# A transformer block on one core: ten fill products give way to 194 products of 28 rows and 12 of 32 columns

## The chip, the core and the metric

The kernel runs on one core of one Trainium2 chip. A core has five engines that work side by side: TensorE (PE in the profile; PEld is its loading of weights), VectorE (DVE), ScalarE (ACT), GpSimd (POOL) and SyncE (SP), which here issues DMAs. The metric is the device time of one execution in microseconds (us); less is better. TensorE multiplies a stationary operand (the weights, loaded first, up to 128 rows by 128 columns) with a moving operand of up to 512 columns, and writes into PSUM, which has eight banks of 128 partitions by 512 f32 values.

## What is computed

One block on 2048 tokens of width 448: a conditioning vector gives shifts, scales and gates; then attention with 16 heads of 28, and a gated MLP that mixes tokens with a 2048x2048 matrix.

```python
mod = (silu(c) @ w_mod).reshape(1, 6, 1, -1)
sa, ca, ga, sb, cb, gb = (mod[:, i] for i in range(6))
h = layernorm(x) * (1 + ca) + sa
x = x + ga * A(h, wqkv, wo)               # softmax attention, 16 heads of 28
h = layernorm(x) * (1 + cb) + sb
x = x + gb * B(h, w_in, w_sp, b_sp, w_out) # gelu, layernorm of one half, w_sp over tokens
```

The change lies in the first line of `h`: the layernorm of the first tokens, ahead of everything that TensorE has to do.

## The kernel before

Tokens are worked on in four groups of 512 (four tiles of 128). For each group the normalised tokens are transposed, scaled and shifted into `hT`, split into a high and a low part, and multiplied with the weights for V (`pv`), Q and K (`pq`). Then come the attention over 16 heads (`mt`, row maxima; `st_ps`, scores; `o_ps`, probabilities times V), the output projection and the MLP.

All engines follow the order in which the code is written out; nothing is moved by a scheduler. Each engine takes its instructions in that order and waits for semaphores of the others where data are not there. PSUM banks are handed out by `bank(name)`, which takes the first of the list `banks` and puts it at the end.

At the start (lines as in the profile of before):

- POOL sets constants to zero or one: `wv`, a part of `heapF` and the last columns of `V` (L297 to L299).
- `pe_fill(21, ones)` (L316) is the first thing in TensorE's queue: 21 products of a tile of ones with itself, 128x128, into a bank `wu` that nobody reads. Another one comes a little later.
- Meanwhile VectorE takes the statistics of the first four tiles of x (`ln_stat`, L368), POOL computes the reciprocal deviations `rs` (L166, L167), and VectorE normalises (`xn`, L379).
- `tp_first` (L460) transposes `xn` on TensorE into four banks `tps`. `mod_dot` (L484, L486) sums the conditioning products into `pc`, from which `mod_cols` (L497, VectorE) takes the columns `col_ca` and `col_sa`.
- `h_hi` (L534, ScalarE) applies these columns to the transposed tiles, and `v_step` (L554) multiplies the result.

Four kinds of product matter below. Products of `heapF`, `heapD` and `heapA` are in the type f32r, which takes one pass. Products of `ones`, `P` and `V` are in full f32, where one product leaves two records in the trace. Transpositions are products with a unit matrix. `o_ps` (L775) has 32 output partitions a product; four of them, one for each quarter of the 128 output partitions, stand in a row:

```python
pe.matmul(otile[h][32 * qb : 32 * qb + 32, :], V[:, kt, h, :], ptiles.pop((u, qb)), start=kt == 0, stop=kt == NT - 1)
```

No product of this kernel has fewer than 128 rows.

Of the kernel before, what the change touches and what calls it, by code (L numbers as in the profile page):

```python
# [8 lines left out]
F32 = mybir.dt.float32  # L9
# [80 lines left out]
def tile_adaln_mha_gmlp(ctx, tc, x, wqkv, wo, w_in, w_spT, b_sp, w_out, cT, w_mod, out):  # L90
    nc = tc.nc
    ctx.enter_context(tc.manual_schedule())
    pe, dve, act, pool, sp = nc.tensor, nc.vector, nc.scalar, nc.gpsimd, nc.sync
# [15 lines left out]
    ones = const.tile([128, 128], F32, name="ones")  # L109
# [5 lines left out]
    cols = {}  # L115
# [5 lines left out]
    heapF = dpool.tile([128, 4 * 896], F32R, name="heapF", tag="heapF")  # L121
    dpool.tile([128, 104], F32, name="padD")

    def hview(heap, off, a, b):
        return heap[:, off : off + a * b].rearrange("p (a b) -> p a b", b=b)
# [104 lines left out]
    V = vpool.tile([128, NT, H, 32], F32, name="V")  # L230
# [12 lines left out]
    banks, mode = list(range(7)), [None]  # L243

    def bank(name):
        k = mode[0](name) if mode[0] else banks[0]
        banks.remove(k)
        banks.append(k)
        return ring.tile([128, 512], F32, name=name, tag=f"b{k}")
# [64 lines left out]
    def pe_fill(n, with_):  # L314
        for _ in range(n):
            pe.matmul(wu[:, 0:128], with_[:, 0:128], ones, start=True, stop=True)  # L316

    accs = {}

    def mod_acc(pair, k):  # L320
# [42 lines left out]
    def ln_stat(g, ts):  # L363
        if g not in mv1:
            mv1[g] = e1.tile([128, 4, 2], F32, name="mv"), e1.tile([128, 4], F32, name="rs")
        for t in ts:
            st = e1.tile([128, 6], F32, name="st", bufs=4)
            dve.bn_stats(out=st, in_=xts[4 * g + t])  # L368
            dve.bn_aggr(out=mv1[g][0][:, t, :], in_=st)
# [82 lines left out]


    tps, fs = {}, {}
    for c in (0, 2, 1, 3):
        tps[c] = bank("tp")

    def tp_first(t, cs=(0, 2, 1, 3)):
        for c in cs:
# [38 lines left out]
                out=cols[nm][:, c : c + 1], in0=pcs[c][:, part * 128 : part * 128 + 1], scalar1=plus1, scalar2=None, op0=ALU.add  # L498
            )

    pe_fill(21, ones)
    ln_stat(0, (0, 1))
    ln_rs(0, 0, 2)
    ln_stat(0, (2, 3))
# [592 lines left out]
    h = H - 1  # L1097
# [49 lines left out]
    heapF = dpool.tile([128, 4 * 896], F32R, name="heapF", tag="heapF")  # L1147
# [260 lines left out]
    for s in range(2):  # L1408
        for six in (False, True):
            prev = None  # L1410
            for n in [n for n in range(s, NP, 2) if PRODUCTS[n][1] or not six]:
                c, _, new, _ = PRODUCTS[n]
# [253 lines left out]
```

## Time and profile before

| | us |
|---|---|
| runs shown (2), lowest and highest | 1376.22, 1376.56 |
| median | 1376.39 |
| profiled execution, span from its first to its last instruction | 1375.3 |
| TensorE busy with products in that span | 1370.1 |
| TensorE's wait for its first operand, at the start | 1.0 |
| ScalarE's wait for the first `xn` (`acc` L471 behind `xn` L379) | 4.5 |

Of the profiled execution the trace gives the span; no other time of it is listed. In the profile an engine's busy time is the union of its instructions. Products overlap on TensorE, so that the record of one is longer than the distance to the next; what a product costs in a dense row is read from the distance of starts. "Idle before" a group is the time in which the engine had nothing to do ahead of it, with the instruction that ended the wait. The chain of waits is followed backwards from the last instruction, at each step to what released it. A window lists, for each engine, its busy time and in brackets the records that fall into it; then the granted clock of TensorE, the share of the DMA engines and their rate.

### The profile page before, as it was taken

The page shows a single profiled execution, that of the slowest core. Times are in us where ns is not written, and L with a number is a line of the kernel's source. Part 1 is how long each engine was busy: PE and PEld are TensorE (multiplying, and loading weights), DVE is VectorE, ACT ScalarE, POOL GpSimd, SP SyncE. Part 2 cuts the span into 40 slices and gives each one's busy share as a digit, 9 for nine tenths or more (in the row PEclk, how much of TensorE's full clock was granted, in tenths as well). Part 3 has the DMA queues.
Part 4 walks back from the last instruction along what each step waited for, and adds up shares of the span by engine and source line. Part 5 has one row for each costly group of instructions (what it writes and reads, how often), then busy time and mean ns, then how long its engine had stood idle before and what let it go on. Part 6 is the DMA issues. An engine that isn't in the chain of part 4 may idle for free.

```text
span 1375.3 us, 20071 instructions
## 1 busy us (share of the span) xinstructions
PE 1370.1 (100%) x7088; PEld 973.9 (71%) x7088; DVE 1069.3 (78%) x1729; ACT 789.5 (57%) x1466; POOL 356.1 (26%) x358
## 2 busy tenths in 40 slices
PE   9999999999999999999999999999999999999998
PEld 8888655555555555555555554888898888888898
DVE  8898888888888888888888880662268798889682
ACT  6623666676767676767777779364234754444221
POOL 2144334243335544633442302200142000000000
PEclk9999999999999999999999999999999999999999
DMA  8464642455244534552343321533202433335842
GB/s 296 138 177 176 187 118 85 109 161 153 69 117 138 151 121 124 156 148 77 110 126 88 96 57 50 174 142 126 85 1 77 130 100 115 115 93 180 270 158 83
DMA packets 93345, 174.65 MB, mean 127 GB/s; under 512 B 17016, under 2 KB 32250, under 8 KB 90698
## 3 DMA queue, kind: packets, MB, share of 16 engines
q1 hardware_dynamic: 90526, 169.07, 40.9%
q10 hardware_dynamic: 2718, 4.30, 0.9%
q8 instruction: 56, 0.92, 0.3%
q14 instruction: 45, 0.37, 0.1%
HBM read 111.71 MB, written 56.82 MB: 123 GB/s over the span
## 4 chain that ended last, share of the span: by engine, by line
PE 97%; DVE 1%; ACT 0%; issue 0%; DMA 0%; POOL 0%; DVEq 0%; ACTq 0%
PE st_ps L760 19%; PE acc L1442 19%; PE o_ps L775 17%; PE mt L728 17%; PE z_ps L1334 5%; PE z_ps L1166 5%; PE pq L415 4%; PE wo_ps L1031 3%; PE y_ps L1522 2%; PE y_ps L1521 2%; PE y_ps L1520 2%; PE pv L397 2%; PE tp L193 1%; DVE st L368 0%; PE pv L554 0%
## 5 line engine op out<-in xcount | busy, mean ns | idle before, releaser
L733 DVE TENSOR_REDUCE pm<-mt 128x1 f32<-128x512 f32 x1024 | 631.3, 682 | 85.9 <-PE mt L728 85.8
L764 ACT ACTIVATE P<-st_ps 128x512 f32<-128x512 f32 x1024 | 514.4, 630 | 201.8 <-PE st_ps L760 201.8
L760 PE MATMUL st_ps<-qst,kst 128*128 128x512 f32 x1024 | 404.3, 406 | 0.0
L728 PE MATMUL mt<-kst,qst 128*128 128x512 f32 x1024 | 402.5, 393 | 0.1
L760 PEld LDWEIGHTS st_ps<-qst,kst 128*128 128x128 f32 x1024 | 191.2, 188 | 141.4 <-issue 93.1
L775 PE MATMUL o_ps<-P,V 128*32 128x512 f32 x2048 | 247.1, 598 | 0.0
L1442 PE MATMUL acc<-wsp_h,heapA 128*128 128x512 f32 x752 | 231.5, 389 | 0.0
L728 PEld LDWEIGHTS mt<-kst,qst 128*128 128x128 f32 x1024 | 192.4, 188 | 32.0 <-POOL kst L665 0.5
L882 POOL TENSOR_TENSOR ws_raw<-ws_raw 128x512 f32<-128x512 f32 x124 | 159.3, 1288 | 195.7 <-DMA ws_scr<-ws_raw 138.9
L1442 PEld LDWEIGHTS acc<-wsp_h,heapA 128*128 128x128 f32 x752 | 141.1, 188 | 29.2
L1442 PE MATMUL acc<-wsp_l,heapA 128*128 128x512 f32 x376 | 146.3, 389 | 0.0
L775 PEld LDWEIGHTS o_ps<-P,V 128*32 128x32 f32 x2048 | 54.7, 109 | 122.9 <-issue 114.6
L1222 ACT ACTIVATE wsp_h<-raw_sp 128x512 fp32r<-128x512 f32 x104 | 65.6, 632 | 125.7 <-PE acc L1442 111.2
L143 DVE TENSOR_TENSOR wsp_l<-raw_sp,wsp_h 128x512 fp32r<-128x512 f32 x104 | 70.4, 687 | 16.6 <-ACT wsp_h L1222 16.4
L1442 PEld LDWEIGHTS acc<-wsp_l,heapA 128*128 128x128 f32 x376 | 70.6, 188 | 14.7
L415 PE MATMUL pq<-heapD,heapD 128*128 128x512 f32 x196 | 61.8, 390 | 0.0
L1338 DVE BATCH_NORM_STATS2 stz<-z 128x6 f32<-128x448 f32 x32 | 19.9, 626 | 44.6 <-ACT z L1337 44.5
L143 DVE TENSOR_TENSOR heapA<-z,heapA 128x1536 fp32r<-128x1536 f32 (+2 forms) x25 | 39.9, 1605 | 6.6 <-ACT heapA L1257 6.5
L1337 ACT ACTIVATE z<-z_ps 128x448 f32<-128x448 f32 x32 | 17.4, 543 | 47.4 <-PE z_ps L1334 47.4
L415 PEld LDWEIGHTS pq<-heapD,heapD 128*128 128x128 f32 x196 | 36.7, 188 | 7.4
L804 POOL TENSOR_TENSOR osb<-osb,rb 128x512 f32<-128x512 f32 x15 | 19.3, 1287 | 85.6 <-DMA rb<-r_scr 80.8
L1521 PE MATMUL y_ps<-wouts,uT 128*128 128x448 f32 x112 | 40.9, 365 | 0.0
(231 smaller groups left out, 1432.1 us busy)
## 6 DMA issues: line engine op xcount, KB each, us to landing
ws_scr<-ws_raw SPq DMA_DIRECT2D x92, 256.0 KB
raw_sp<-ws_scr SPq DMA_DIRECT2D x92, 256.0 KB
ws_raw<-in_w_spT_dram SPq DMA_DIRECT2D x72, 256.0 KB
kst<-qk_scr SPq DMA_DIRECT2D x45, 224.0 KB
qst<-qk_scr SPq DMA_DIRECT2D x45, 224.0 KB
qk_scr<-qh SPq DMA_DIRECT2D x28, 256.0 KB
qk_scr<-ql SPq DMA_DIRECT2D x28, 256.0 KB
z_scr<-z1t SPq DMA_DIRECT2D x28, 256.0 KB
```

The lines of the kernel that those rows point to most:

```text
L143: eng.tensor_tensor(out=dst, in0=a, in1=hi.bitcast(F32), op=ALU.subtract)
L415: pe.matmul(pq, wqk[:, b, m * 128 : (m + 1) * 128], hT[g][:, a, :], start=j == 0, stop=j == NST - 1)
L728: pe.matmul(mt, qst[h % 3][:, t * 128 : (t + 1) * 128], kst[h % 3][:, kb * 512 : (kb + 1) * 512], start=True, stop=True)
L733: dve.tensor_reduce(out=pms[h][:, t, kb : kb + 1], in_=mt, axis=AX.X, op=ALU.max)
L760: pe.matmul(st, kst[h % 3][:, kt * 128 : (kt + 1) * 128], qst[h % 3][:, qb * 512 : (qb + 1) * 512], start=True, stop=True)
L764: act.activation(p, st, AF.Exp, scale=SCALE)
L775: pe.matmul(otile[h][32 * qb : 32 * qb + 32, :], V[:, kt, h, :], ptiles.pop((u, qb)), start=kt == 0, stop=kt == NT - 1)
L882: pool.tensor_tensor(out=ws_tile(op[0]), in0=ws_tile(op[2]), in1=ws_tile(op[4]), op=ALU.add if op[3] == "+" else ALU.subtract)
L1166: pe.matmul(ps_t, w1[:, b, f * 128 : (f + 1) * 128], h2T[g][:, a, :], start=j == 0, stop=j == NST - 1)
L1334: pe.matmul(ps_t[:, :D], h2T[g][:, a, tt * 128 : (tt + 1) * 128], w2[:, b, hf * D : (hf + 1) * D], start=j == 0, stop=j == NST - 1)
L1442: pe.matmul(a[j], z[:, c], w, start=start and k == 0, stop=st == 3 and k == 2, skip_group_check=not new or j == 3)
L1521: pe.matmul(y[:, :D], uT[k][:, 7 + f, ts], wouts[0][:, f, :], start=False, stop=False)
```

## The change

Three things change, all at the start.

Two memsets are added to POOL's queue: 1024 columns of `heapF` to 0.5, and the first 512 columns of `V` to 1.0. Both places are written again later, by the weights for Q and K and by the first V tile.

`pe_fill(21, ones)` becomes `pe_fill(11, ones)`, and behind it stands `probe()`, whose results nobody reads. It takes four banks and issues, from those constants:

- 24 fours of products of 28 rows, 128 weight columns and 512 moving columns, type f32r. The i-th of a four takes partitions 32i to 32i+27 and writes bank i.
- Three times: four products of 32 output partitions in full f32 (`cols`, with the weights and the moving operand from `V`, all 128 rows), then six more fours.
- Two products of 28 rows and 256 columns, on the third and fourth quarter, then six more fours.

Then the list of banks is set so that the transpositions get the banks that they had.

```diff
+    pr = hview(heapF, 0, 2, 512)
+    pool.memset(heapF[:, 0:1024].bitcast(F32), 0.5)
+    pool.memset(V[:, 0, :, :], 1.0)
+
+    def probe():
+        pt = [bank("probe") for _ in range(4)]
+
+        def mm(k, i, rows, src):
+            r = slice(rows * i, rows * i + (28 if rows == 32 else rows))
+            pe.matmul(pt[k], src[r, 0, 0:128], src[r, 1, :], start=True, stop=True)
+
+        def quads(n, src):
+            for _ in range(n):
+                for i in range(4):
+                    mm(i, i, 32, src)
+
+        def cols():
+            for half in range(1):
+                for i in range(4):
+                    pe.matmul(pt[0][32 * i : 32 * i + 32, :], pv[:, 0:32], pv, start=True, stop=True)
+
+        pv = V[:, 0:2, :, :].rearrange("p a h d -> p (a h d)")[:, 0:512]
+        quads(24, pr)
+        for _ in range(3):
+            cols()
+            quads(6, pr)
+        for i in (2, 3):
+            r = slice(32 * i, 32 * i + 28)
+            pe.matmul(pt[i][:, 0:256], pr[r, 0, 0:128], pr[r, 1, 0:256], start=True, stop=True)
+        for _ in range(6):
+            for i in (0, 1, 2, 3):
+                mm(i, i, 32, pr)
+
...
     tps, fs = {}, {}
-    for c in (0, 2, 1, 3):
-        tps[c] = bank("tp")
...
-    pe_fill(21, ones)
+    pe_fill(11, ones)
+    probe()
+    banks[:] = [1, 2, 3, 4, 5, 6, 0]
+    for c in (0, 2, 1, 3):
+        tps[c] = bank("tp")
     ln_stat(0, (0, 1))
```

TensorE's queue from its start to the first product of the V weights, before (line, operation, output and inputs, shape of the output, count; `wu` is the fill bank, `tp` the transposed x, `pc` the conditioning sums):

```order
L316 MATMUL wu<-ones 128x128 x21
L460 MATMUL tp<-ident,xn 128x128 x8
L484 MATMUL pc<-silu,wm 128x2
L486 MATMUL pc<-ones,acc 128x128 x2
L460 MATMUL tp<-ident,xn 128x128 x8
L316 MATMUL wu<-ones 128x128
```

The same place now, up to the first transpositions; line numbers behind the new function are higher by 31 or more:

```order
L316 MATMUL wu<-ones 128x128 x11
L327 MATMUL probe<-heapF 128x512 x96
L337 MATMUL probe<-V 32x512 x4
L327 MATMUL probe<-heapF 128x512 x24
L337 MATMUL probe<-V 32x512 x4
L327 MATMUL probe<-heapF 128x512 x24
L337 MATMUL probe<-V 32x512 x4
L327 MATMUL probe<-heapF 128x512 x24
L346 MATMUL probe<-heapF 128x256 x2
L327 MATMUL probe<-heapF 128x512 x24
L491 MATMUL tp<-ident,xn 128x128 x8
```

The 206 products stand between the fill and the first transposition. The first `probe` product of `heapF` and the first of `V` each wait for POOL, and the first transposition into each bank now also waits for the product that wrote the bank before it.

POOL's queue at the same place, the one piece of the difference that isn't a line number:

```order
 L298 MEMSET heapF 64x896
 L299 MEMSET V 128x256x4
+L319 MEMSET heapF 128x1024
+L320 MEMSET V 128x512
 L166 TENSOR_SCALAR rs<-mv 128x2
 L167 TENSOR_TENSOR rs<-rs,mhalf 128x2
```

The two memsets stand ahead of the first reciprocal deviation `rs`. The queues of VectorE, ScalarE and SyncE keep their order.

## The prediction

> **What bounds the kernel now.** I read the page first, for the engine that carries the end:
>
> ```profile
> span 1375.3 us, 20071 instructions
> PE 1370.1 (100%) x7088; PEld 973.9 (71%) x7088; DVE 1069.3 (78%) x1729; ACT 789.5 (57%) x1466; POOL 356.1 (26%) x358
> PE 97%; DVE 1%; ACT 0%; issue 0%; DMA 0%; POOL 0%; DVEq 0%; ACTq 0%
> ```
>
> TensorE (PE) is 97% of the chain that ended last. Whatever makes it later early on comes out at the end nearly whole, unless a wait behind that place takes it up. So only the place of the change matters, the first microseconds. The timeline there, PE first, then its weight loads (PEld), POOL and ScalarE (columns: start, length, engine, line, output and inputs, count, idle before and its releaser):
>
> ```profile
> 8.00 1.34 PE L460 MATMUL tp<-ident,xn 128*128 128x128 f32 x8
> 9.18 0.28 PE L484 MATMUL pc<-silu,wm 128*128 128x2 f32 x2
> 9.47 0.71 PE L486 MATMUL pc<-ones,acc 128*128 128x128 f32 x4
> 10.02 1.06 PE L460 MATMUL tp<-ident,xn 128*128 128x128 f32 x8
> ...
> 8.57 0.53 PEld L460 LDWEIGHTS tp<-ident,xn 128*128 128x128 f32 x5 [0.33 <-ACT xn L389]
> ...
> 2.71 0.96 POOL L299 MEMSET V<- 128x1024 f32 x1
> 6.08 0.24 POOL L166 TENSOR_SCALAR rs<-mv 128x2 f32<-128x2 f32 x1 [2.42 <-DVE mv L369]
> ...
> 10.69 0.78 ACT L534 ACTIVATE heapD<-tp,col_sa,col_ca 128x512 fp32r<-128x512 f32 x1
> ```
>
> Until 8.00 us PE only runs fill products (L316) while the first rows of x are loaded and normalised; the first useful work is the transposition `tp` at 8.00. The first result that needs PE is read by ScalarE at 10.69. The chain of waits over the first 30 us, cut to its links there, says who waits then:
>
> ```profile
> 7.45 0.41 DVE xn L379
> 8.57 0.76 PE tp L460 x5
> 9.47 0.71 PE pc L486 x4
> 10.18 0.48 PE tp L460 x4
> 10.69 0.79 ACT heapD L534
> ...
> 23.96 1.88 DVE heapF L143 x3
> ```
>
> Up to 8.57 VectorE and ScalarE hold the end, then PE, ScalarE and later VectorE alternate. All of their work behind 10.2 waits, directly or in its queue, for the columns that come out of `pc`. A later PE at 8.00 therefore moves all three together.
>
> **The change, part by part.** It removes ten of the 21 leading fill products, puts two memsets on POOL, and puts 206 products ahead of the first `tp`: 192 of 28 rows and 512 columns in 48 fours, 2 of 256 columns, and 12 of 32 output partitions in three groups of four (the change's words count the 194 of 28 rows). Bank order and all later work stay.
>
> *When the new work starts.* A product in full f32 leaves two records: 22 fill products (21 and a later one), 44 records in the groups of instructions. Two windows of them that open at 1.00 and close just before and behind a start:
>
> ```profile
> L316 PE MATMUL wu<-ones 128*128 128x128 f32 x44 | 7.5, 347 | 1.0 <-DVE ones L110 1.0
> ...
> 1.00:5.65 4.65, 4.61 (x21) 4.62 (x22) 1.00 0.75 229
> 1.00:5.70 4.70, 4.66 (x22) 4.67 (x23) 1.00 0.75 230
> ```
>
> The 22nd record, the last of eleven products, starts at about 5.67 and streams some 0.11 us (the 14 transpositions below: 0.10 each), so PE is free at 5.78. POOL's first new memset has 128x1024 elements like the one at 2.71, 0.96 us, and ends near 4.6; the second is half that, ends near 5.1, ahead of POOL's next work at 6.08. The memsets cost nothing; their cover is that gap of 2.42 us on POOL, and without it `rs` and the first `xn` would be about 1.5 us late, which the new PE work hides anyway.
>
> *One product, one weight load.* In the chain of waits, two dense stretches; in the timeline, transpositions, and weight loads beside products of two columns:
>
> ```profile
> 1047.91 255.69 PE acc L1442 x1128
> ...
> 27.64 1.69 PE L193 MATMUL tp<-ident,xn 128*128 128x128 f32 x14
> 29.08 0.94 PE L415 MATMUL pq<-heapD,heapD 128*128 128x512 f32 x3
> ...
> 12.14 0.53 PEld L486 LDWEIGHTS pc<-ones,acc 128*128 128x128 f32 x4
> L1442 PEld LDWEIGHTS acc<-wsp_h,heapA 128*128 128x128 f32 x752 | 141.1, 188 | 29.2
> ```
>
> A product of 512 columns in the one-pass type takes 255.69 / 1128 = 0.227 us, its load of 128 weight columns hidden. The transpositions take (29.08 - 27.64) / 14 = 0.103 us. Loads follow each other every (0.53 - 0.19) / 3 = 0.11 us.
>
> *What a four costs.* No product of before uses fewer than 128 rows, so this is not in the trace. The nearest rows are `o_ps`, which splits the array by columns instead, in fours of 32 output partitions. Products and weight loads around one such stretch:
>
> ```profile
> 150.55 0.40 PE L728 MATMUL mt<-kst,qst 128*128 128x512 f32 x1
> 150.88 1.92 PE L775 MATMUL o_ps<-P,V 128*32 128x512 f32 x16
> 152.73 0.50 PE L760 MATMUL st_ps<-qst,kst 128*128 128x512 f32 x1
> 153.07 0.39 PE L728 MATMUL mt<-kst,qst 128*128 128x512 f32 x1
> ...
> 150.88 0.16 PEld L775 LDWEIGHTS o_ps<-P,V 128*32 128x32 f32 x8 [0.25 <-PE st_ps L760]
> 151.33 0.13 PEld L775 LDWEIGHTS o_ps<-P,V 128*32 128x32 f32 x4 [0.30 <-issue]
> 151.76 0.13 PEld L775 LDWEIGHTS o_ps<-P,V 128*32 128x32 f32 x4 [0.30 <-issue]
> ```
>
> Four loads fit into 0.13 us though each lasts 0.11, and a round of four records comes every 151.76 - 151.33 = 0.43 us, or 0.11 a record (a group of four products of the change is two such rounds): four quarters of the array load and compute at once. Bounds for a four of 28 rows are therefore 0.227 us (all at once, loads hidden) and 4 x (0.227 + 0.11) = 1.35 us (one after the other, loads bare). It cannot be a gain: no four streams its 512 columns faster than one product. I take 0.227, since `o_ps` is the nearest row: also quarters, also other operands and outputs for each, also long runs.
>
> *What a switch costs.* Ahead of `o_ps` the first load comes 0.33 behind the start of the last full product, so 0.10 more than 0.227; four rounds (1.72) end in a full product 1.85 behind their start, 0.13 more; that product's weights lie bare, 153.07 - 152.73 = 0.34, 0.11 more.
>
> The sum on PE, from the first load at 5.78 + 0.10 = 5.88:
> - weights 0.11, 24 fours x 0.227 = 5.45: 5.56 us;
> - three times: drain 0.10, two rounds and their end 0.86 + 0.13, weights 0.11, six fours 1.36: 3 x 2.56 = 7.68;
> - the two half products put two quarters half a product ahead: 0.11; six fours 1.36: 1.47. Out of step each quarter still gets its next product as it ends, so I charge no more;
> - drain and weights to the first `tp`: 0.21.
>
> In all 14.9 us: `tp` starts at 20.8 in place of 8.00, 12.8 later. Behind it two waits go, since all inputs are there by then: 0.33 before 8.57, and most of the 0.29 between the starts at 9.18 and 9.47, together 0.6. ScalarE at 10.69 and VectorE's queue behind it are late next, by 12.2. No later idle stretch of theirs waits for something that isn't itself moved. The removed fill products save nothing: from 5.78 to 8.00 PE would have waited.
>
> The profiled span of 1375.3 lies 1.1 below the median of two runs, 1376.39, which is what lies around it. So 1376.39 + 12.2 = **1388.6 us**, 0.9% slower, within the 2% that a measurement here can tell from no change.
>
> **The rivals.**
>
> *The fours are fed one load or one instruction at a time.* If the four loads of 128 columns queue up, a four takes 4 x 0.11 = 0.44: 48 x 0.213 = 10.2 more, 1398.8. The fastest sustained issue on PE that I find is the 14 transpositions, 28 instructions in 1.44 us, 0.051 each; eight at that pace are 0.41, 1397.4. For it: loads of 128 columns are four times as long as those of `o_ps`, and such pace over hundreds of instructions stands in no row. Against it: at 150.88 eight loads went out in 0.16.
>
> *Loads lie bare within each quarter.* If a quarter cannot load while its own product runs, a four takes 0.227 + 0.11: 48 x 0.11 = 5.3 more, 1393.9. Against it: full products hide their loads (188 ns within 227), and so do the quarters of `o_ps`. The Trainium skill's "TensorE: Matmul & The Clock Gate" (Part 3, The mechanism) states just this, that a weight load overlaps running matmuls only where the row group differs; those rows disagree, for full rows. The same page (Measured speedup vs the span model) gives 3.07 times for four row tiles: as an estimate 4 x 0.227 / 3.07 = 0.296 a four, which would make the sum 1391.9; no run here shows it yet.
>
> *The fours run one after the other.* This is the one on the other side. If quarters by rows don't compute at once, a four is 4 x 0.227 = 0.908 and 48 x 0.681 = 32.7 more: 1421.3, slower by 3.3%; bare loads make it 1442. It decides from 0.55 us a four on ((27.5 - 12.2) / 48 = 0.32 above mine). For it: four results of 128 partitions each must leave at once, four times what `o_ps` writes. Against it: nothing but the likeness to `o_ps`.
>
> *The slow clock stays.* The first 22 records took 4.6 us, 0.21 each, though the window shows a granted clock of 1.00; in this one stretch the array ran at half speed:
>
> ```profile
> 5.60:7.90 2.30, 2.30 (x23) 2.30 (x21) 1.00 0.97 362
> ```
>
> From 5.60 on, records come about twice as fast (some 21 in 2.30). If quarter-height work counts as idle, fours cost 0.43 and the column rounds double: 48 x 0.2 + 2.6 = 12.2 more, 1400.8. `o_ps` keeps its speed for 700 us, against it.
>
> **How the numbers follow.** Forecast (all at once) 0.47; bare loads 0.08; one load or instruction at a time 0.22; slow clock 0.03; one after the other 0.17, its bare form included; anything else 0.03. The forecast's own range is 1386 to 1391 (switches of 0 to 0.3 us at eight places, up to 1.5 us of stalls taken up). Low end 1386; the high end goes to 1402 to hold the feeding and clock rivals, 0.80 together; what is left out is the serial case. Faster by over 2% 0.01, for nothing is taken away that PE waited for; within 2% 0.80; slower 0.19.
>
> **What would show it.** In the profile after: the starts of the `probe` products in the first 24 fours (four within a few hundredths, next four 0.227 later: right; 0.11 apart: fed singly; 0.227 apart: serial); the same behind each column group and out of step; eight records of 32 columns in about 0.99; `tp` near 20.8; the ScalarE activation of `tp` 2.1 behind it; then everything shifted by one amount. Wrong are the sum if fours in a row slow down as they go on or stay slow behind the column products, and the pass-through if the shift shrinks between 25 and 60 us.

## The result

| | before, us | changed, us |
|---|---|---|
| runs shown, lowest to highest | 1376.22 to 1376.56 | 1388.14 to 1388.27 |
| median | 1376.39 | 1388.2 |
| profiled execution, span | 1375.3 | 1386.5 |

The ratio is 1.0086, with a 95% interval of 1.0057 to 1.0116: 11.8 us slower, and by the 2% bound no change. The profiled execution of the changed kernel took 1388.27 us, its span is 1.8 shorter.

The profile's page of the changed kernel gives, for the lines that the prediction shows of the kernel before:

```profile
span 1386.5 us, 20470 instructions
PE 1381.4 (100%) x7286; PEld 981.0 (71%) x7286; DVE 1069.0 (77%) x1729; ACT 789.6 (57%) x1466; POOL 357.3 (26%) x360
```

TensorE is busy 11.3 us longer and the span is 11.2 longer; VectorE and ScalarE do the same work as before. Of the 399 new instructions, 396 are records of products and of weight loads on TensorE. The timeline of the changed kernel, TensorE first, then POOL and the first reader:

```profile
5.31 5.75 PE L327 MATMUL probe<-heapF 28*128 28x512 f32 x96
10.99 1.06 PE L337 MATMUL probe<-V 128*32 128x512 f32 x8
11.99 1.67 PE L327 MATMUL probe<-heapF 28*128 28x512 f32 x24
13.59 1.06 PE L337 MATMUL probe<-V 128*32 128x512 f32 x8
14.59 1.67 PE L327 MATMUL probe<-heapF 28*128 28x512 f32 x24
16.18 1.07 PE L337 MATMUL probe<-V 128*32 128x512 f32 x8
17.18 1.88 PE L327 MATMUL probe<-heapF 28*128 28x512 f32 x26
18.68 0.28 PE L346 MATMUL probe<-heapF 28*128 28x256 f32 x2
18.80 1.54 PE L327 MATMUL probe<-heapF 28*128 28x512 f32 x22
20.27 1.09 PE L491 MATMUL tp<-ident,xn 128*128 128x128 f32 x8
...
4.52 0.52 POOL L320 MEMSET V<- 128x512 f32 x1
6.09 0.23 POOL L166 TENSOR_SCALAR rs<-mv 128x2 f32<-128x2 f32 x1 [1.05 <-DVE mv L402]
...
22.51 0.78 ACT L569 ACTIVATE heapD<-tp,col_sa,col_ca 128x512 fp32r<-128x512 f32 x1 [12.08 <-PE tp L491]
```

The first row of 24 fours and the switch behind it last from 5.31 to 10.99. Without the switch (0.10) and the first bare weights (0.11), as the prediction prices them, that is 5.47 / 24 = 0.228 a four, the time of a single product: the four quarters compute at once. A block (column group and six fours) takes 13.59 - 10.99 = 2.60, the next 2.59. From the first new product to the first transposition it is 20.27 - 5.31 = 14.96 us. POOL had both memsets done at 5.04 and began `rs` at 6.09, as before. ScalarE waits 12.08 us for `tp` and starts at 22.51 instead of 10.69.

So the time comes from one place, and it is passed on. Three stretches of the chain of waits began at 23.96, 61.71 and 1047.91 before; the second of them, and then all three in the changed kernel:

```profile
61.71 9.99 PE pq L415 x44
```

```profile
35.81 1.88 DVE heapF L143 x3
73.56 9.99 PE pq L448 x44
1059.05 255.69 PE acc L1477 x1128
```

They are later by 11.85, 11.85 and 11.14. Of the 0.7 us that are missing in the last, 0.6 went in the output projection and the transpositions within it. Pieces of its chain before, then the same pieces in the changed kernel, where the line has another number:

```profile
866.10 27.68 PE wo_ps L1031 x134
895.31 4.53 PE wo_ps L1031 x22
```

```profile
877.82 27.15 PE wo_ps L1066 x134
906.50 4.47 PE wo_ps L1066 x22
```

From the first of these pieces to the end of the projection's last one this stretch took one of two lengths, 0.6 apart, in every profile of this study: the longer in the kernel before and in two variants that keep the change (256 columns, runs of four), the shorter in the other eleven. So it isn't the change that decides it; what does stays open.

### The profile page after: what moved, and what is told of

It reads as the page before. It is cut to its first block, busy times and chain, and to the rows that moved or that the text cites. A ratio compares the mean times of both kernels' runs of the same rounds, so it can differ in the third digit from the quotient of the medians.

```text
span 1386.5 us, 20470 instructions
## 1 busy us (share of the span) xinstructions
PE 1381.4 (100%) x7286; PEld 981.0 (71%) x7286; DVE 1069.0 (77%) x1729; ACT 789.6 (57%) x1466; POOL 357.3 (26%) x360
## 4 chain that ended last, share of the span: by engine, by line
PE 98%; DVE 1%; ACT 0%; issue 0%; POOL 0%; DVEq 0%; ACTq 0%
PE st_ps L795 19%; PE acc L1477 18%; PE o_ps L810 17%; PE mt L763 17%; PE z_ps L1369 5%; PE z_ps L1201 5%; PE pq L448 4%; PE wo_ps L1066 3%; PE y_ps L1557 2%; PE y_ps L1555 2%; PE pv L430 2%; PE y_ps L1556 2%; PE probe L327 1%; PE tp L193 1%; DVE st L401 0%; PE pv L589 0%
```

## The experiments

The theory: the four quarters of the array compute and load weights at once; the new products put off the first transposition by their own length, and everything behind it moves along. All variants keep the rest of the changed kernel. Single runs are read by the profile, by the stretch from the first `probe` product to the first `tp` product: it took 14.96 and 15.00 us in two profiles of the changed kernel, whose whole runs lie up to 1.5 us apart.

**The changed kernel again, and the same lateness from other work.**

> The changed kernel once more, beside the three others. Both theories: 1388.2 us, 11.8 above the kernel before, with the first transposition near 20.3 if the clock rises near 4.5 us and near 20.8 if it rises near 5.6.

```diff
-    pe_fill(11, ones)
-    probe()
+    pe_fill(11 + 67, ones)
```

> In place of the 206 products stand 67 more fill products (134 records of 0.112 us, 15.0 us), the memsets stay: the first transposition is about as late, by other work. Theory (the time comes from this lateness alone): 1388.2, within 0.6. Rival (a part comes from what the new products leave behind, such as their banks and the waits for them): nearer to the kernel before by that part, over 1 us below the changed kernel.

Beside the same seven runs of the kernel before (median 1375.49), the changed kernel took 1388.32 (ratio 1.0091, 1.0074 to 1.0108) and the one with fill products alone 1388.2 (1.0092, 1.0077 to 1.0107). So the changed kernel was 12.8 us above the kernel before this time, not 11.8: a difference between two sets of runs is good to about 1 us. The timeline of the variant with fill products alone:

```profile
1.04 19.16 PE L316 MATMUL wu<-ones 128*128 128x128 f32 x156 [1.04 <-DVE ones L110]
20.04 1.04 PE L491 MATMUL tp<-ident,xn 128*128 128x128 f32 x8
```

The first transposition at 20.04, put off by quite another kind of product, gives the same time. The lateness is the cause; the banks of the new products and the waits for them add nothing that shows beside a scatter of 1 us. In the changed kernel's second profile the products began at 5.72 rather than 5.31 and the first transposition at 20.72.

**All on one quarter.**

```diff
-                    mm(i, i, 32, src)
+                    mm(0, 0, 32, src)
...
-                mm(i, i, 32, pr)
+                mm(0, 0, 32, pr)
```

> All four products of a four stand on the first quarter and write its bank. Theory (four quarters of the array compute at once; on one quarter products follow each other): a four takes 4 x 0.227 = 0.908 us, 48 x 0.681 = 32.7 more than the changed kernel, 1420.9. Rival (a product of 28 rows is short by itself, some 0.057, wherever it stands): no change, 1388.2.

1462.65 us: the rival falls, since products on one quarter follow each other (0.227 us each in the first 3 us). But the theory gave 42 us less, and these need another cause. Windows of TensorE in this run (busy time and records, then the granted clock, DMA share and rate):

```profile
5.70:8.50 2.80, 2.80 (x13) 1.00 0.98 360
8.90:20.00 11.10, 11.10 (x28) 0.50 0.47 188
44.00:92.00 48.00, 47.94 (x125) 0.50 0.00 0
92.00:97.00 5.00, 5.00 (x25) 0.50 0.20 52
97.00:110.00 13.00, 13.00 (x72) 0.98 0.58 192
```

The granted clock fell to 0.50 some 3 us after the row began, though TensorE was never idle; from then on a product took 11.1 / 26 = 0.427 us in place of 0.227. The clock stayed there through the column groups, and came back 5.5 us after the first transposition, which came at 91.95. That is 39.0 later than the theory has it (20.27 + 32.7), and the slow stretch behind it cost 2 us more: 41 of the 42. This is the mechanism of the prediction's rival on the slow clock, in a place where it wasn't looked for. One thing is left open: in this variant and in those below, the products of one quarter also write one and the same bank, so that it isn't shown whether they wait for the quarter or for the bank.

**The first row alone on one quarter.**

```diff
-        quads(24, pr)
+        for _ in range(96):
+            mm(0, 0, 32, pr)
```

> Only the first row of 96 products stands on one quarter; all behind it is that of the changed kernel. Theory (one busy quarter counts as idle to the clock, four quarters count as work): the granted clock falls to 0.50 some 3 us into the row (13 products at 0.227, 83 at 0.427: 38.4 us, 33 more than 24 fours) and rises again some 5 us behind it, while fours and column groups run: 2.7 more, about 1424. Rival (products of 28 rows hold the clock down however many quarters work, once it is down): 0.50 up to the first full products and about 5 us into them, some 1433.

1422.92 us. The timeline, and windows of the same run:

```profile
6.03 38.36 PE L327 MATMUL probe<-heapF 28*128 28x512 f32 x96
44.32 1.94 PE L337 MATMUL probe<-V 128*32 128x512 f32 x8
46.19 2.42 PE L327 MATMUL probe<-heapF 28*128 28x512 f32 x24
48.54 1.06 PE L337 MATMUL probe<-V 128*32 128x512 f32 x8
```

```profile
6.95:10.30 3.35, 3.35 (x16) 1.00 1.02 376
10.34:12.00 1.66, 1.66 (x6) 0.50 1.09 425
40.00:44.00 4.00, 4.00 (x11) 0.50 0.00 0
46.00:48.00 2.00, 2.00 (x24) 0.53 0.00 0
48.00:50.00 2.00, 2.00 (x28) 1.00 0.00 0
```

The clock fell 4.3 us after the row began, where it was 3.0 with all on one quarter. In both runs that is some 3.4 us after the records of TensorE had come to follow each other twice as fast, at about 6.9 and 5.3 (see the start, below). It came back at 47.9, within the fours: 1.7 us after they began and 3.6 after the column group ahead of them did. The rival, that work of 28 rows holds the clock down however many quarters work, falls. That fours count as work by themselves is shown better by the longer row below, 27.5 us of nothing else at full pace.

**Two quarters.**

```diff
-                    mm(i, i, 32, src)
+                    mm(i % 2, i % 2, 32, src)
...
-                mm(i, i, 32, pr)
+                mm(i % 2, i % 2, 32, pr)
```

> A four stands on the first and second quarter in turn, two products on each. Theory: two at once, 2 x 0.227 = 0.454 a four, 48 x 0.227 = 10.9 more than the changed kernel, 1399.1. Rival (what counts is that neighbours in the queue differ in quarter): 0.227 a four, 1388.2.

1399.55 us. Its timeline at the first row and at the first transposition:

```profile
5.11 11.19 PE L327 MATMUL probe<-heapF 28*128 28x512 f32 x96
...
31.00 1.09 PE L491 MATMUL tp<-ident,xn 128*128 128x128 f32 x8
```

From the first product to the first transposition it is 25.89 in place of 14.96: 10.9 more, as the theory has it. The granted clock of the run is 1.000: two busy quarters suffice.

**Each quarter's products side by side.**

```diff
-            for _ in range(n):
-                for i in range(4):
+            for _ in range(n // 2):
+                for i in (0, 0, 1, 1, 2, 2, 3, 3):
                     mm(i, i, 32, src)
...
-        for _ in range(6):
-            for i in (0, 1, 2, 3):
+        for _ in range(3):
+            for i in (0, 0, 1, 1, 2, 2, 3, 3):
                 mm(i, i, 32, pr)
```

> The same products, but each quarter's two stand side by side: 0, 0, 1, 1, 2, 2, 3, 3. Theory (products start in the order of the queue, a waiting one holds up all behind it): eight products take four steps of 0.227, 0.454 a four, 48 x 0.227 = 10.9 more, 1399.1. Rival (the queue lets a product of a free quarter pass a waiting one): 0.227 a four, 1388.2.

1388.16 us: here the theory fell and the rival held. The timeline shows the first row and the first transposition:

```profile
5.72 5.76 PE L327 MATMUL probe<-heapF 28*128 28x512 f32 x96
...
20.72 1.09 PE L491 MATMUL tp<-ident,xn 128*128 128x128 f32 x8
```

The row is as fast as one of fours (5.75), and the whole takes 15.0. A product of a free quarter starts although an earlier product is still waiting for its own quarter: products of different quarters (and banks) do not start in the order in which they stand.

**Runs of 24 and of 6, and runs of four.**

```diff
-            for _ in range(n):
-                for i in range(4):
+            for i in range(4):
+                for _ in range(n):
                     mm(i, i, 32, src)
```

> The products of one quarter stand in a run: 24 on the first, 24 on the second and so on; in the blocks behind the column groups 6 and 6. Theory A (a product of a free quarter may pass any waiting one within reach of a long queue): four quarters still work at once, 1388.2. Theory B (it passes only one or two waiting ones): nearly one quarter at a time, 16.3 more for the first row and 3 x 4.1 for the blocks, 1416.8, and up to 25 more where the clock falls as it did with one quarter. Between them: runs of 6 as fast as fours, runs of 24 not.

1438.53 us: theory A falls, and by its time the run lies where theory B has it with its up to 25 us for the clock. The products follow each other every 0.427 us from the start, at half speed like the first fill products of every run (0.213 us a record, later 0.112); one-quarter work took over before the speed had risen, and it didn't rise while that work lasted. (The granted clock is shown as 1.00 here, as at every start.) What may be passed can be read from the pattern all the same. Windows of this run, of the products of 28 rows:

```profile
6.60:14.70 8.10, 8.10 (x20) 6.19 (x19) 1.00 0.93 361
14.72:16.20 1.48, 1.48 (x9) 1.36 (x8) 1.00 0.00 0
16.60:23.40 6.80, 6.80 (x18) 5.20 (x16) 1.00 0.00 0
23.42:24.90 1.48, 1.48 (x9) 1.36 (x8) 1.00 0.04 11
```

For 8.10 us one quarter works alone, then for 1.5 us two do, then one again. The first quarter's products start at 6.03, 6.63 and then every 0.427; at 14.73 its 21st starts, and with it the first of the next quarter. Three of the first quarter (22nd to 24th) are still waiting then: the queue goes on behind three waiting products, where theory B had one or two. In the runs of 6, which come behind the first column group, the next quarter begins at 45.58 with the third, again three before the end.

```diff
-        quads(24, pr)
+        for _ in range(6):
+            for i in (0, 0, 0, 0, 1, 1, 1, 1, 2, 2, 2, 2, 3, 3, 3, 3):
+                mm(i, i, 32, pr)
```

> The first row's 96 products stand in runs of four, 0, 0, 0, 0, 1, 1, 1, 1 and so on; all behind it is that of the changed kernel. Theory (each quarter has a line of its own in which one product runs and three wait, and the queue stops only where a line is full, as the runs of 24 and of 6 showed it): no run of four fills a line for long, four quarters stay at work, 15.0 us from the first product to the first transposition, 1388.2. Rival (three waiting products in all may be passed): the third run is held up, about two quarters at once, 0.45 a four, 5.4 more, 1393.6.

1389.3 us; the one run of the kernel before beside it took 1376.9, so it's 12.4 above. The row lasts 6.17 in place of 5.75, the whole 15.4:

```profile
5.49 6.17 PE L327 MATMUL probe<-heapF 28*128 28x512 f32 x96
11.59 1.06 PE L337 MATMUL probe<-V 128*32 128x512 f32 x8
```

That is 0.4 us for a row that the rival made 5.4 longer; where the 0.4 went isn't shown. The rival falls, and both runs fit the theory that each quarter has a line of its own with room for one running and three waiting products.

**A longer row.**

```diff
-        quads(24, pr)
+        quads(120, pr)
```

> The first row of fours is 120 long in place of 24: 960 instructions in a row. Theory (the pace is the array's and lasts): 96 x 0.227 = 21.8 more, 1410.0. Rival (instructions or weights are fed more slowly once the queue has run dry, at 0.051 us an instruction as the transpositions show it, 0.41 a four): up to 96 x 0.41 = 39.4 more, 1427.6.

1411.25 us:

```profile
6.03 27.61 PE L327 MATMUL probe<-heapF 28*128 28x512 f32 x480
...
42.85 1.09 PE L491 MATMUL tp<-ident,xn 128*128 128x128 f32 x8
```

The first transposition follows 36.82 us behind the first product: 21.9 more for 96 fours, 0.228 each. The pace lasts, and so does the clock.

**Narrower products.**

```diff
-            pe.matmul(pt[k], src[r, 0, 0:128], src[r, 1, :], start=True, stop=True)
+            pe.matmul(pt[k][:, 0:256], src[r, 0, 0:128], src[r, 1, 0:256], start=True, stop=True)
```

and the same with 128 in place of 256. The two half products stay as they are.

> All products of 28 rows have 256 columns in place of 512. Theory (the array's streaming sets the pace, loads run beside it, four at once): 0.11 to 0.12 a four, 48 x 0.107 = 5.1 less than the changed kernel, 1383.1. Rival (eight instructions a four cannot be issued faster than the 0.028 us each that the changed kernel shows): 0.227 stays, 1388.2.

> All products of 28 rows have 128 columns. Theory: streaming would take 0.06, but a load of 128 columns takes 0.11 on its quarter, so a four takes 0.11 to 0.12 as with 256 columns, 1383. Rival 1 (loads run fully beside, nothing else binds): 0.06 to 0.07, 48 x 0.16 = 7.7 less, 1380.5. Rival 2 (issue binds at 0.028 us an instruction): 0.227, 1388.

1383.24 and 1382.47 us. Windows in the first row, with 256 and then with 128 columns:

```profile
6.40:9.00 2.60, 2.60 (x96) 2.60 (x90) 1.00 1.02 371
```

```profile
6.70:9.00 2.30, 2.30 (x92) 2.30 (x84) 1.00 1.02 382
```

A window also counts records that only reach into it, two or three fours here. By the starts within it a four takes 0.120 with 256 columns and 0.111 with 128. A quarter of 0.227, which streaming 128 columns would take, is 0.06. The time of a load of 128 weight columns, 0.11, fits as the bound, with four quarters loading at once. That the queue just reaches its own limit there, eight instructions in 0.111 or 0.014 each, wasn't tested; against it, the four products start within 4 ns of each other and then none for a tenth of a microsecond, where a limit on single instructions would spread them.

**No column groups.**

```diff
         for _ in range(3):
-            cols()
             quads(6, pr)
```

> The three groups of 32 columns are left out, all fours stay. Theory (a group costs drain 0.10, its two rounds and their end 0.99, and bare weights 0.11 of the four behind it): 3 x 1.20 = 3.6 less than the changed kernel, 1384.6. Rival (fours behind a group are slower for a while than fours in a long row): more than 3.6 less, by 18 fours x what each is slower.

1385.23 us:

```profile
6.03 10.09 PE L327 MATMUL probe<-heapF 28*128 28x512 f32 x168
...
17.54 1.09 PE L490 MATMUL tp<-ident,xn 128*128 128x128 f32 x8
```

From the first product to the first transposition it is 11.5 us, 3.5 less than in the changed kernel: 1.15 a group where 1.20 was reckoned. This row began while TensorE was still at half speed, though: its second four starts 0.585 behind the first, in the changed kernel 0.335. With these 0.25 us added it is 1.23 a group, which is also what a block of 2.60 leaves beside six fours. The rival, at 18 fours, has no more than 0.1 us left for it in all.

## Why the prediction held

The forecast was 1388.6 us, the measured median is 1388.2. The mechanism was right, and so were its large terms. That the totals agree to 0.4 us is in part luck: the runs of the kernel before spread from 1375.0 to 1376.9 in this study, and beside another set of them the change cost 12.8. Term by term, by the first profile:

| term | predicted, us | changed kernel, us |
|---|---|---|
| first product | 5.88 | 5.31 |
| first product to first transposition | 14.9 | 14.96 |
| one four | 0.227 | 0.228 |
| one block of a column group and six fours | 2.56 | 2.60 and 2.59 |
| first transposition | 20.8 | 20.27 |
| waits that go behind it | 0.6 | 0.45 |
| lateness that is passed on | 12.2 | 11.8 |

- *A four costs one product's time.* Right, and for the reason given, the likeness to `o_ps`: on one quarter the same products follow each other, on two they take twice as long (10.9 us more, as reckoned), and 120 fours in a row keep the pace. The feeding rival was excluded by the long row and by the eight instructions in 0.111. (It called a load of 128 columns four times as long as one of `o_ps`. That holds for the columns; the time of a record is 188 ns against 109.) The rival of bare loads fell too: a four of 0.228 has no room for a load of 0.11 beside a product of 0.227, so a quarter loads while its own product runs. The trace does not agree with the sentence of the Trainium skill on which that rival drew ("TensorE: Matmul & The Clock Gate", Part 3, The mechanism), that a load overlaps running products only where the row group differs. Nor does it agree with the 3.07 times of the Trainium skill (the same page, Measured speedup vs the span model): a long row reaches 4 x 0.227 / 0.228, nearly four.
- *Switches.* Right in size; a column group with both its switches was 1.23 where the sum had 1.20.
- *Out of step.* Right within 0.05: from the third column group at 16.18 to the first transposition it is 4.09, where the sum has 2.46 (a block without its first drain) + 1.47 + 0.21 = 4.14. Two of the last 24 products start ahead of the half products, so that the rows of the timeline do not part them.
- *The start.* Off by 0.57, by chance. The profile before had TensorE's records come twice as fast from about 5.6 us on; in the profiled run of the changed kernel that came at about 4.5:

```profile
1.00:4.50 3.50, 3.46 (x16) 3.46 (x17) 1.00 0.71 234
4.60:5.20 0.60, 0.60 (x7) 0.59 (x6) 1.00 0.99 266
```

The same kernel's second profile had its first product at 5.72. The moment varies from run to run, and 0.57 us go with it.
- *What is passed on.* Right: 11.8 us at the first reader, 11.85 at 73 us. The spans differ by 11.2, mostly because of the two lengths of the projection.
- *The slow clock.* It was no danger for fours, as forecast; that the same products on one quarter would meet it was not foreseen, and cost the forecast for that variant 41 us.

## What to carry to other kernels

On a kernel whose chain is nearly all one engine, work put ahead of its first useful instruction costs its own length, less the time for which that engine would have waited. Two very different kinds of work cost the same here. Products of few rows are worth their price only if several quarters of the array are kept at work: four cost what one costs, while on one quarter alone each costs a whole product, and later twice that, by the clock. The quarters need not alternate strictly, as long as no quarter has more than three products waiting ahead of another's.

## What was not expected of the hardware

- One busy quarter (28 of 128 rows) counts as idle to the clock: granted 0.50 after 3.0 and 4.3 us of it, a product at 0.427 us, back up after 1.9 us of a column group and 1.7 us of fours, or after 5.5 us of full products. Two busy quarters kept 1.00 over 26 us. Whether it is the rows or the share of the array that counts was not tried.
- Products of different quarters, with a bank for each, start out of the queue's order: past one waiting product without loss, past three of a quarter at most. Nothing here tells whether they also end out of order for a reader who waits on the last of them.
- The moment at which TensorE's records come to follow each other twice as fast lay between about 4.0 and 6.9 us in these profiles (not within 60 us in the runs of 24 and 6), with the granted clock shown as 1.00 throughout; only the distance of records shows it.
